# Spectral layer and two feed-forward layers on one core: the second mixing unit in three float32r passes, four weight conversions in the forward transform, odd groups reordered

## The chip, the cores and the metric

The kernel runs on one core of a Trainium2 chip. The metric is the device time of one execution in microseconds (us); a program that is run several times is told by the median.

## What is computed

```python
X = np.fft.rfft(x, axis=1)                       # x: (2, 3008, 256), float32
Yr = Xr @ w_r - Xi @ w_i + b_r
Yi = Xr @ w_i + Xi @ w_r + b_i
Yr, Yi = soft_threshold(Yr, 0.01), soft_threshold(Yi, 0.01)
y = np.fft.irfft(Yr + 1j * Yi, n=3008, axis=1)   # (2, 3008, 256) -> 6016 tokens
h = y @ w_in1;  y = (h * sigmoid(1.702 * h)) @ w_out1     # w_in 256x2048
h = y @ w_in2;  y = (h * sigmoid(h)) @ w_out2             # w_out 2048x256
```

The four feed-forward weights arrive as 64-bit floats; the kernel reads them as 64-bit integers and turns them into 32-bit floats itself.

## The kernel before, in words

Everything is 32-bit arithmetic. A matrix product on TensorE is made in one of two ways. *Full precision* multiplies float32 by float32 and appears as two records for one matmul. *Three passes* splits both operands into a rounded float32r part (hi) and the rest (lo) and adds hi·hi, hi·lo and lo·hi, one record each.

**Forward transform.** The input is folded by symmetry into sums and differences before it is multiplied with cosine and sine matrices. Sixteen *groups* (`groups`, numbers 0 to 15) stand for (parity of the input q, batch b, matrix t): 0 to 3 are even rows with t 0 and 1, 4 to 11 odd rows with t 0 to 3 for both batches, 12 to 15 even rows with t 2 and 3. A raw tile of the input (512 KB, `load_raw`, L300; nine in pool `raw`, three more in pieces) gives two *half sums* by a wide add of VectorE (`halves`, L313, 128x512; `keep` for even rows, `lv` for odd ones), and each of these two folded tiles (`fold`, L332, 128x256, narrow adds; some are combined once more at L346). `fwd_mm` (L394) or `fwd_pair` (L428) multiplies, `fwd_evac` moves the result from PSUM to the tiles xt: by ScalarE copies (L446), for groups 12 to 15 by a ScalarE copy eo (L450) and four VectorE adds (L461, L462). `fold` runs three groups ahead of the products.

**Mixing.** Twelve *units* (`mids`, 0 to 11) multiply xt by the weights w_r and w_i. Units below the table entry n32 (2 before) use full precision (L572); the others use three passes (L575), with the weights split into wh and wl (L556, L557, just behind the forward transform) and each unit's xt split into xh (a ScalarE cast, L507) and xl (a ScalarE product with -1, L503, to which a DMA of the GpSimd queue adds xt, L504), both made by `xsplit`. A bias row is added by one more matmul (L578). VectorE and ScalarE combine and threshold the result (L584 to L618).

**Inverse transform** (L394 as psi, `inv_post`), then two feed-forward layers in blocks of 1024 tokens, eight groups to a block: L876 multiplies with w_in, the activation runs on ScalarE (L879), L848 multiplies with w_out. At a change of block `xsums` and `xprep` make the seven operand combinations of the next block from yt; L796 is one of them, a VectorE subtraction that reads yt.

**Conversion of a weight.** A piece is loaded as raw 64-bit values (L162, L163; pool buffer `raw`, one), ScalarE takes the upper halves (cv_c, L180; one buffer), VectorE makes five bit operations (L185 to L189), a DMA of the GpSimd queue adds the low part (L190), and then the next raw load is issued. `window` puts ScalarE's step in the program, `pump` the rest. When a later window finds a converted piece, it *places* it: four small VectorE sums (L218 to L221) and hi/lo splits on ScalarE and by DMA (L105 to L107). Table entries say where windows stand: `tf` in the forward transform by group, `tm` in the mixing by unit, `ti` in the inverse transform by step; `pl` lists the steps of the inverse transform that place a held piece. Before, ten pieces are converted ahead of the feed-forward layers: three, six and one.

The order on every engine is that of the program text; a table `CFG` at the top sets who does what and when.

```python
        if g == 10:
            xsplit(N('n32'), 1)
        if g in N('tf'):
            tick(N('tf').count(g))
```

Of the kernel before, what the change touches and what calls it, by code (L numbers as in the profile page):

```python
# [9 lines left out]
F32 = mybir.dt.float32  # L10
CFG = {'lv0': 'V', 'lv': 'V', 'dd0': 'VPVVPPPPPVVP', 'dd': 'V', 'ths': 'VVVVPV', 'thf': 'V', 'ivf': 'V', 'cva': 'P', 'pol': 'PPPP', 'pil': 'P', 'mvl': 'PVVP', 'xl': 'V', 'xse': 'V', 'gl': 'VPPPPPPP', 'tf': [6, 10, 13], 'tm': [0, 2, 4, 6, 8, 10], 'ml': [], 'pk': 6, 'ti': [3], 'pi': 4, 'pl': [1, 4, 8, 10, 13], 'kb': [0, 1, 1, 1, 1, 1, 1, 0], 'kr': [0, 1, 0, 1, 0, 1, 1, 0], 'fa': 3, 'xp': [2, 4, 4, 5], 'xq': [1, 4, 1], 'xs': 4, 'xi': [7, 7, 9, 10, 10, 11, 8], 'xsi': 9, 'xo': (0, 1, 6, 2, 3, 4, 5), 'xd': (0, 1, 4, 6), 'ca': 4, 'tl': True, 'fwd': 'all', 'rest0': 'all', 'rest1': 'all', 'last1': 'all', 'inv': 'all', 'mid': 'all', 'last0': 'all', 'thm': 'A', 'gl0': 'PVPVVVPV', 'gl2': 'PPPPPPPP', 'gl3': 'PPPPPPPV', 'xl0': 'VVVVVPV', 'xl1': 'V', 'pre': 13, 'pre2': 0, 'yd': 6, 'lvb': 6, 'mlp': 'all', 'pr': 'V', 'pf': 'V', 'eo': '0111', 'n32': 2, 'li': [3, 5, 7], 'lii': [0], 'xa': 4, 'nhb': 6, 'ddb': 6, 'mlp1': 'all', 'mlp2': 'all'}
# [45 lines left out]
def spectral_mlp_kernel(ctx, tc, xin, mfwd, minv, wc, bias, w_in1, w_out1, w_in2, w_out2, outT):  # L57
# [60 lines left out]
    m_tiles = {}  # L118
    m_order = [("f", q, t) for q, t in ((0, 0), (0, 1), (1, 0), (1, 1), (1, 2), (1, 3), (0, 2), (0, 3))] + [("i", q, t) for q in range(2) for t in (0, 2)]

# [48 lines left out]
    def cv_bits(raw, n):  # L169
        w = raw.bitcast(U32).rearrange("p (n t) -> p n t", t=2)  # L170
        hf = raw.bitcast(F32).rearrange("p (n t) -> p n t", t=2)[:, :, 1]
        c = cv_p.tile([P, 2 * CU], F32, tag="c", name="cv_c", bufs=1)
        if n < 4:
            a = cv_p.tile([P, 2 * CU], F32, tag="a", name="cv_a", bufs=3)
        elif n == 4:
# [17 lines left out]
        return a, c  # L193
# [85 lines left out]
    m0_p = opened("m0", "left", 4)  # L279
    raw_p = opened("raw", "left", 3)  # L280
    lv_p = opened('lv', 'left', N('lvb'))
    xs_p = opened("xs", "left", 18)
    groups = [(0, b, cs) for b in range(B) for cs in range(2)]
    groups += [(1, b, t) for b in range(B) for t in range(4)]
    groups += [(0, b, 2 + cs) for b in range(B) for cs in range(2)]
# [16 lines left out]
    def halves(q, b, j, cs):  # L302
# [6 lines left out]
        else:  # L309
            lv = lv_p.tile([P, 2, D], F32, tag="lv", name="lv")  # L310
        lvs[q, b, cs, j] = lv
# [3 lines left out]
    def fold(g):  # L315
# [6 lines left out]
        for j in range(NJ):  # L322
            if t == 0:
                halves(q, b, j, 0)
            lv = lvs[q, b, cs, j]
# [23 lines left out]
    def fold_pair(g):  # L349
        q, b, _ = groups[g]  # L350
        for j in range(NJ):
# [15 lines left out]
    def prep_wc():  # L367
# [156 lines left out]
    for g, (q, b, t) in enumerate(groups):  # L524
# [244 lines left out]
    def xsums(l, i):  # L769
# [3 lines left out]
        E('xse', 1).tensor_sub(b12, b22, b12)  # L773

    def xprep(l, i, k, part=3):

# [7 lines left out]
        if part & 2:  # L784
# [79 lines left out]
    def group(l, i, p, hook):  # L864
# [116 lines left out]
    for at, (l, i, p) in enumerate(seq):  # L981
# [10 lines left out]
        def hook(h):  # L992
            if more:
                if h == 1:
                    xprep(*nxt, 0)
                if h == 3:
                    xprep(*nxt, 1)
                    xprep(*nxt, 2)
                    xprep(*nxt, 3, 1)
                if h == 4:  # L1000
                    xprep(*nxt, 3, 2)
            if p == 0 and (l, i) != (0, 0):
                for x in {1: (4,), 3: (6, 5)}.get(h, ()):
                    xprep(l, i, x)
# [169 lines left out]
```

## Time and profile before

| | |
|---|---|
| median of 3 runs | 1150.15 us (1149.65 to 1151.89) |
| profiled execution | 1149.84 us |
| its span, first to last instruction | 1148.0 us |
| TensorE busy (matmul) | 1138.8 us, 99% |
| ScalarE, VectorE, GpSimd busy | 774.1, 615.5, 475.9 us |
| forward transform until | about 59.6 us |
| mixing | about 59.6 to 130.6 us |
| inverse transform | about 130.6 to 172.8 us |
| feed-forward layers | the rest |

A row of the timeline gives start, duration, engine, line and operation; several instructions of one kind are merged with their count. In square brackets stands how long the engine was idle before and what ended that.

### The profile page before, as it was taken

Reading aid. Unit: us, or ns where it says so; the run is one execution under the profiler, and the core shown is the slowest. Engines: PE = TensorE matmul, PEld = TensorE weight load, DVE = VectorE, ACT = ScalarE, POOL = GpSimd, SP = SyncE. Lnnn points to the kernel's source line nnn. Section 1 sums busy time; section 2 is a strip of 40 time slices with the busy share of each in tenths; the row PEclk is TensorE's granted clock in tenths of the full one; section 3 lists DMA queues with packets and bytes.
Section 4 is the critical chain, followed back from the end, with each engine's and each line's share of the span. In section 5 each row is a group of like instructions: output and inputs, shape, how many; then the busy total and the mean of one; then the engine's idle time right before and its main releaser. Section 6 shows DMA issues by size and latency. Waiting matters only on the chain.

```text
span 1148.0 us, 14644 instructions
## 1 busy us (share of the span) xinstructions
PE 1138.8 (99%) x5094; PEld 946.3 (82%) x5094; DVE 615.5 (54%) x1015; ACT 774.1 (67%) x1445; POOL 475.9 (41%) x410
## 2 busy tenths in 40 slices
PE   8999999999999999999999999999999999999998
PEld 6768987878888888888889878888888888888897
DVE  8889997764565465564554633533523523523422
ACT  2587357877677676686677776765765866757655
POOL 0253164443444444444447646433334433344333
PEclk9999999999999999999999999999999999999999
DMA  8699494431121212112211000010000100100100
GB/s 306 176 185 238 114 161 86 105 72 37 49 62 37 74 37 59 52 38 74 52 41 37 28 28 19 1 38 1 20 18 1 37 1 1 38 1 1 37 1 33
DMA packets 39852, 68.69 MB, mean 60 GB/s; under 512 B 3681, under 2 KB 16225, under 8 KB 39778
## 3 DMA queue, kind: packets, MB, share of 16 engines
q1 hardware_dynamic: 26306, 45.51, 12.2%
q0 software_dynamic: 13472, 22.24, 11.4%
q8 instruction: 40, 0.66, 0.2%
q14 instruction: 34, 0.28, 0.1%
HBM read 35.15 MB, written 10.35 MB: 40 GB/s over the span
## 4 chain that ended last, share of the span: by engine, by line
PE 93%; DVE 2%; ACT 2%; issue 1%; DMA 1%; SPq 0%; POOL 0%; DVEq 0%; ACTq 0%; POOLq 0%
PE o L848 43%; PE x L876 37%; PE psm L575 5%; PE psi L394 4%; PE psf L394 3%; PE psm L572 1%; ACT yt L879 1%; DMA xr<-in_x 1%; ACT g L881 0%; DVE keep L313 0%; DVE tmp L796 0%; ACT yt L895 0%; ACT x L783 0%; DVE x L790 0%; SPq L485 0%
## 5 line engine op out<-in xcount | busy, mean ns | idle before, releaser
L886 POOL TENSOR_TENSOR g<-yt,g 128x512 fp32r<-128x512 f32 (+1 forms) x282 | 363.6, 1301 | 498.2 <-PE x L876 306.3
L848 PE MATMUL o<-g,wo 128*128 128x512 f32 (+1 forms) x2304 | 559.7, 385 | 0.0
L876 PE MATMUL x<-x,wi 128*128 128x512 f32 (+1 forms) x2016 | 498.9, 386 | 2.0 <-ACT yt L895 1.1
L848 PEld LDWEIGHTS o<-g,wo 128*128 128x128 f32 x2304 | 432.5, 188 | 80.6
L876 PEld LDWEIGHTS x<-x,wi 128*128 128x128 f32 x2016 | 377.5, 188 | 77.1 <-ACT yt L895 3.2
L879 ACT ACTIVATE yt<-yt 128x512 f32<-128x512 f32 (+1 forms) x288 | 179.1, 622 | 264.2 <-DVE yt L926 217.3
L881 ACT CAST g<-yt 128x512 fp32r<-128x512 f32 (+1 forms) x384 | 235.0, 612 | 12.2
L926 DVE TENSOR_TENSOR yt<-yt,x 128x512 f32<-128x512 f32 (+1 forms) x96 | 64.8, 675 | 217.7 <-PE x L876 217.3
L898 DVE TENSOR_TENSOR yt<-yt,x 128x512 f32<-128x512 f32 (+1 forms) x96 | 65.0, 677 | 175.0 <-ACT yt L895 173.1
L886 DVE TENSOR_TENSOR g<-yt,g 128x512 fp32r<-128x512 f32 (+1 forms) x102 | 70.0, 686 | 71.9 <-ACT g L881 71.9
L190 POOL DMA_DIRECT2D cv_a<-cv_c x32 | 28.1, 878 | 112.4 <-DVE cv_c L189 106.0
L930 DVE TENSOR_TENSOR yt<-yt,x 128x512 f32<-128x512 f32 (+1 forms) x96 | 64.9, 676 | 0.0
L790 DVE TENSOR_TENSOR x<-yt,x 128x512 fp32r<-128x512 f32 (+1 forms) x55 | 47.6, 866 | 31.5 <-ACT x L783 31.5
L895 ACT COPY yt<-x 128x512 f32<-128x512 f32 (+1 forms) x96 | 54.9, 572 | 1.7 <-DVE tmp L796 0.9
L879 ACT ACTIVATE yt<-x 128x512 f32<-128x512 f32 (+1 forms) x96 | 56.0, 584 | 0.0
L916 ACT COPY yt<-x 128x512 f32<-128x512 f32 (+1 forms) x96 | 55.9, 582 | 0.1
L914 ACT COPY yt<-x 128x512 f32<-128x512 f32 (+1 forms) x96 | 54.9, 572 | 1.4 <-PE x L876 1.4
L394 PE MATMUL psi<-m,f 128*128 128x188 f32 (+3 forms) x224 | 45.2, 357 | 0.0
L394 PEld LDWEIGHTS psi<-m,f 128*128 128x128 f32 x224 | 37.6, 190 | 5.5
L394 PE MATMUL psf<-m,xf 128*128 128x190 f32 (+2 forms) x176 | 36.2, 367 | 1.4 <-ACT xt L446 0.8
L394 PEld LDWEIGHTS psf<-m,xf 128*128 128x128 f32 x176 | 29.6, 190 | 8.3 <-ACT xt L446 1.3
L783 ACT CAST x<-yt 128x512 fp32r<-128x512 f32 (+1 forms) x59 | 36.4, 617 | 0.0
(120 smaller groups left out, 804.8 us busy)
## 6 DMA issues: line engine op xcount, KB each, us to landing
raw<-in_wi SPq DMA_DIRECT2D x32, 256.0 KB, 3.6
cv_a<-cv_c POOLq DMA_DIRECT2D x32, 256.0 KB, 5.0
raw<-in_wo SPq DMA_DIRECT2D x16, 512.0 KB, 3.9
xl<-xt POOLq DMA_DIRECT2D x20, 256.0 KB, 8.0
out_t<-yt SPq DMA_DIRECT2D x20, 256.0 KB, 2.0
raw<-in_x SPq DMA_DIRECT2D x9, 512.0 KB, 5.6
wi<-tmp POOLq DMA_DIRECT2D x8, 256.0 KB, 4.7
w_in<-cv_a SPq DMA_DIRECT2D x8, 256.0 KB, 2.0
```

The source lines that it names most:

```text
L394: nc.tensor.matmul(ps, hi[:, c : c + P], m[:, k, :w], start=i == 0, stop=i == last)
L575: nc.tensor.matmul(t, st, mv, start=n == 0 and k == 0, stop=n == 3 and grp == 1 and k == 2)
L848: nc.tensor.matmul(acc[h, mm], st, mv, start=first and k == 0, stop=last and k == 2)
L876: nc.tensor.matmul(ps, st, mv, start=first and m == 0, stop=m == 2, skip_group_check=True)
L879: nc.scalar.activation(g, g if src is None else src, func)
L881: nc.scalar.copy(gh, g)
L886: eng.tensor_sub(gl, g, r32(gh))
L895: nc.scalar.copy(y1, X)
L898: nc.vector.tensor_add(y1, y1, Y)
L916: nc.scalar.copy(y3, X)
L926: nc.vector.tensor_add(y2, y2, X)
L930: nc.vector.tensor_add(y3, y3, Z)
```

## The change

- `n32` goes from 2 to 1: unit 1 is made in three passes; its xl is made at group 10, and unit 2's xl and unit 1's xh behind wh and wl.
- `tf` goes from [6, 10, 13] to [6, 10, 12, 14], `ti` from [3] to []: four conversions in the forward transform, six in the mixing, none in the inverse transform. `pl` goes from [1, 4, 8, 10, 13] to [1, 4, 8, 9, 11, 13].
- Groups 4 to 11 run with t in the order 0, 2, 1, 3, and the matrices are loaded so. The half sums of t = 0 and t = 1 are made in the group that first uses them; the second is written over its raw tile. Pool `raw` has 5 buffers for 3, `lv` 3 for 6. Raw tiles are loaded ahead of the matrices, the ninth at group 4.
- The bias' lower part is written in place.
- At a change of block one subtraction (`xfifth`, before L796) moves ahead of the add that completes y3; the table of Silu is loaded by an instruction of its own.

```diff
-    m_order = [("f", q, t) for q, t in ((0, 0), (0, 1), (1, 0), (1, 1), (1, 2), (1, 3), (0, 2), (0, 3))] + ...
+    m_order = [("f", q, t) for q, t in ((0, 0), (0, 1), (1, 0), (1, 2), (1, 1), (1, 3), (0, 2), (0, 3))] + ...
...
-    raw_p = opened("raw", "left", 3)
-    lv_p = opened('lv', 'left', N('lvb'))
+    raw_p = opened("raw", "left", 5)
+    lv_p = opened('lv', 'left', 3)
...
-    groups += [(1, b, t) for b in range(B) for t in range(4)]
+    groups += [(1, b, t) for b in range(B) for t in (0, 2, 1, 3)]
...
-            lv = lv_p.tile([P, 2, D], F32, tag="lv", name="lv")
+            lv = raws[q, b, j][1] if cs else lv_p.tile([P, 2, D], F32, tag="lv", name="lv")
...
-            if t == 0:
-                halves(q, b, j, 0)
+            if q == 1 and t < 2:
+                halves(q, b, j, t)
...
-            if t == 0:
-                halves(q, b, j, 1)
-                del raws[q, b, j]
-                if (q, b) == (0, 0):
-                    load_raw()
...
-    load_raw(3)
+    load_raw(6)
+    load_m()
+    load_m()
+    load_raw(2)
     fold_pair(0)
-    load_m()
     fold_pair(2)
-    load_m()
...
-    load_raw(3)
...
+        if g == 4:
+            load_raw()
...
-            xsplit(N('n32'), 1)
+            xsplit(1, 1)
...
     nc.vector.tensor_sub(wl, wc_s, r32(wh))
+
+    xsplit(2, 1)
+    xsplit(1, 0)
...
-    hold.insert(2, hold.pop())
+    hold[2:] = hold[4:] + hold[2:4]
...
+    def xfifth(l, i, src=None):
+        (b11, _), (b21, _) = xhalves(i)
+        nc.vector.tensor_sub(xtmp[0], b21, b11 if src is None else src)
...
-            if k == 3:
-                nc.vector.tensor_sub(xtmp[0], b21, src)
+            if k == 3 and not begun:
+                xfifth(l, i, src)
...
         nc.vector.tensor_add(y2, y2, X)
+        hook(7)
         g22 = gate(1, 1, y2)
...
+                if h == 7:
+                    xfifth(*nxt)
...
+            if (l, i, p, h) == (1, 0, 0, 1):
+                nc.scalar.preload_act_table(AF.Silu)
```

How the order moves, at three places. First ScalarE at the end of the forward transform. Of the kernel before, from the third conversion's first step (`cv_c<-raw_548`) to the fourth's (`cv_c<-raw_630`):

```order
L180 ACTIVATE cv_c<-raw_548 128x512
L105 ACTIVATE wi_609<-cv_a 128x384
L107 CAST wi_609<-cv_a 128x384
L105 ACTIVATE wi_609<-tmp 128x512
L107 CAST wi_609<-tmp 128x512
L450 COPY eo<-psf 128x2x188 x3
L556 CAST wh<-wc_s 128x1536
L503 ACTIVATE xl<-xt_303 128x512
L503 ACTIVATE xl<-xt_304 128x512
L507 CAST xh<-xt_97 128x512
L507 CAST xh<-xt_98 128x512
L180 ACTIVATE cv_c<-raw_630 128x512
```

Of the change, from the evacuation of groups 12 and 13 on (line numbers are those of the changed file; `cv_c<-raw_607` is the fourth conversion, xt_97 and xt_98 belong to unit 2, xt_95 and xt_96 to unit 1):

```order
L443 COPY eo<-psf 128x2x188 x2
L180 ACTIVATE cv_c<-raw_607 128x512
L105 ACTIVATE wi_642<-cv_a 128x384
L107 CAST wi_642<-cv_a 128x384
L105 ACTIVATE wi_642<-tmp 128x512
L107 CAST wi_642<-tmp 128x512
L443 COPY eo<-psf 128x2x188 x2
L550 CAST wh<-wc_s 128x1536
L496 ACTIVATE xl<-xt_97 128x512
L496 ACTIVATE xl<-xt_98 128x512
L500 CAST xh<-xt_95 128x512
L500 CAST xh<-xt_96 128x512
```

The fourth conversion's first step stood behind wh, xl and xh; now it stands ahead of them and of the last two eo copies.

Second, VectorE at the same place. Of the kernel before, the evacuation of group 15, wl, and then the fourth conversion:

```order
L461 TENSOR_TENSOR xt_310<-psf,eo 128x256
L462 TENSOR_TENSOR xt_314<-psf,eo 128x2x60
L436 TENSOR_TENSOR xt_312<-eo,psf 128x256
L436 TENSOR_TENSOR xt_314<-eo,psf 128x2x60
L557 TENSOR_TENSOR wl<-wc_s,wh 128x1536
L218 TENSOR_TENSOR tmp<-cv_a 128x128
L219 TENSOR_TENSOR tmp<-cv_a 128x128
L220 TENSOR_TENSOR tmp<-tmp,cv_a 128x128
L221 TENSOR_TENSOR tmp<-cv_a,tmp 128x128
L185 TENSOR_SCALAR cv_c<-cv_c 128x512
L186 TENSOR_SCALAR cv_c<-cv_c 128x512
L187 SCALAR_TENSOR_TENSOR cv_a<-raw_630,cv_c 128x512
```

Of the change, the end of the fourth conversion, groups 14 and 15, and wl:

```order
L187 SCALAR_TENSOR_TENSOR cv_a<-raw_607,cv_c 128x512
L188 TENSOR_SCALAR cv_c<-cv_a 128x512
L189 SCALAR_TENSOR_TENSOR cv_c<-raw_607,cv_c 128x512
L454 TENSOR_TENSOR xt_303<-psf,eo 128x256
L455 TENSOR_TENSOR xt_307<-psf,eo 128x2x60
L429 TENSOR_TENSOR xt_305<-psf,eo 128x256
L429 TENSOR_TENSOR xt_307<-psf,eo 128x2x60
L454 TENSOR_TENSOR xt_304<-psf,eo 128x256
L455 TENSOR_TENSOR xt_308<-psf,eo 128x2x60
L429 TENSOR_TENSOR xt_306<-eo,psf 128x256
L429 TENSOR_TENSOR xt_308<-eo,psf 128x2x60
L551 TENSOR_TENSOR wl<-wc_s,wh 128x1536
```

wl stood ahead of the fourth conversion; now it stands behind it and behind the two evacuations.

Third, VectorE at the first change of block (the two adds into yt complete y2 and y3 of the last group of a block). Of the kernel before:

```order
L926 TENSOR_TENSOR yt<-yt,x 128x512
L930 TENSOR_TENSOR yt<-yt,x 128x512
L886 TENSOR_TENSOR g<-yt,g 128x512
L790 TENSOR_TENSOR x<-yt,x 128x512
L796 TENSOR_TENSOR tmp<-yt 128x512
L898 TENSOR_TENSOR yt<-yt,x 128x512
```

Of the change:

```order
L927 TENSOR_TENSOR yt<-yt,x 128x512
L774 TENSOR_TENSOR tmp<-yt 128x512
L932 TENSOR_TENSOR yt<-yt,x 128x512
L887 TENSOR_TENSOR g<-yt,g 128x512
L791 TENSOR_TENSOR x<-yt,x 128x512
L899 TENSOR_TENSOR yt<-yt,x 128x512
```

The subtraction into tmp (L796, now L774) goes ahead of y3's add and the two instructions behind that.

## Rows read from the trace of the kernel before

**Rows 1.** The page's head: TensorE's busy time; granted clock of forty slices, in tenths.

```profile
PE 1138.8 (99%) x5094; PEld 946.3 (82%) x5094; DVE 615.5 (54%) x1015; ACT 774.1 (67%) x1445; POOL 475.9 (41%) x410
...
PEclk9999999999999999999999999999999999999999
```

**Rows 2.** TensorE's waits over the span: us in total, times, longest us.

```profile
PE x L876 <- ACT yt L895: 1.1, 3, 0.7
PE warm L472 <- DVE neglam L474: 1.1, 1, 1.1
```

**Rows 3.** The chain that ended last, in the mixing: start us, us, what.

```profile
59.59 3.43 PE psm L572 x8
63.25 6.87 PE psm L572 x16
...
73.79 2.77 PE psm L575 x12
76.79 5.45 PE psm L575 x24
```

**Rows 4.** Timeline of ScalarE, 55 to 68 us.

```profile
55.00 0.68 ACT L180 ACTIVATE cv_c<-raw 128x512 f32<-128x512 f32 x1 [2.54 <-DMA raw<-in_wi]
...
57.44 0.83 ACT L450 COPY eo<-psf 128x376 f32<-128x376 f32 x2
...
60.04 1.48 ACT L556 CAST wh<-wc_s 128x1536 fp32r<-128x1536 f32 x1
...
62.47 1.12 ACT L507 CAST xh<-xt 128x512 fp32r<-128x512 f32 x2
64.64 0.68 ACT L180 ACTIVATE cv_c<-raw 128x512 f32<-128x512 f32 x1 [1.05 <-DMA raw<-in_wi]
...
67.08 0.58 ACT L584 COPY us<-psm 128x512 f32<-128x512 f32 x1
```

**Rows 5.** Timeline of VectorE, third conversion to wl.

```profile
55.71 0.43 DVE L185 TENSOR_SCALAR cv_c<-cv_c 128x512 f32<-128x512 f32 x1
...
58.43 0.42 DVE L461 TENSOR_TENSOR xt<-psf,eo 128x256 f32<-128x256 f32 x1
...
59.47 0.42 DVE L461 TENSOR_TENSOR xt<-psf,eo 128x256 f32<-128x256 f32 x1
...
61.55 1.76 DVE L557 TENSOR_TENSOR wl<-wc_s,wh 128x1536 fp32r<-128x1536 f32 x1
```

**Rows 6.** Timeline of VectorE, folds of group 4 to conversion 2.

```profile
18.78 0.69 DVE L313 TENSOR_TENSOR lv<-raw 128x512 f32<-128x512 f32 x1
...
35.86 0.42 DVE L185 TENSOR_SCALAR cv_c<-cv_c 128x512 f32<-128x512 f32 x1
...
41.19 2.08 DVE L332 TENSOR_TENSOR xf<-keep 128x256 f32<-128x256 f32 x6
44.92 0.29 DVE L218 TENSOR_TENSOR tmp<-cv_a 128x128 f32<-128x128 f32 x1 [1.65 <-DMA cv_a<-cv_c]
...
45.86 0.42 DVE L185 TENSOR_SCALAR cv_c<-cv_c 128x512 f32<-128x512 f32 x1
```

**Rows 7.** Landing times: the page's DMA issues; the tile xl, 30 to 140 us.

```profile
raw<-in_x SPq DMA_DIRECT2D x9, 512.0 KB, 5.6
...
DMA to landing us min/median/max: 3.4/8.0/10.6
```

**Rows 8.** Timelines of TensorE, VectorE and ScalarE at two changes of block.

```profile
255.05 1.79 DVE L796 TENSOR_TENSOR tmp<-yt 128x512 f32<-128x512 f32 x1
...
256.93 0.59 ACT L895 COPY yt<-x 128x512 f32<-128x512 f32 x1 [0.85 <-PE x L876]
...
257.57 0.96 PE L876 MATMUL x<-x,wi 128*128 128x512 f32 x3 [0.69 <-ACT yt L895]
...
658.95 0.96 PE L876 MATMUL x<-x,wi 128*128 128x512 f32 x3 [0.26 <-ACT yt L895]
...
663.04 1.97 PE L876 MATMUL x<-x,wi 128*128 128x512 f32 x6 [0.70 <-ACT yt L916]
```

More of the change, by code (lines that the diff above doesn't have):

```diff
@@ L10 @@
 F32 = mybir.dt.float32
-CFG = {'lv0': 'V', 'lv': 'V', 'dd0': 'VPVVPPPPPVVP', 'dd': 'V', 'ths': 'VVVVPV', 'thf': 'V', 'ivf': 'V', 'cva': 'P', 'pol': 'PPPP', 'pil': 'P', 'mvl': 'PVVP', 'xl': 'V', 'xse': 'V', 'gl': 'VPPPPPPP', 'tf': [6, 10, 13], 'tm': [0, 2, 4, 6, 8, 10], 'ml': [], 'pk': 6, 'ti': [3], 'pi': 4, 'pl': [1, 4, 8, 10, 13], 'kb': [0, 1, 1, 1, 1, 1, 1, 0], 'kr': [0, 1, 0, 1, 0, 1, 1, 0], 'fa': 3, 'xp': [2, 4, 4, 5], 'xq': [1, 4, 1], 'xs': 4, 'xi': [7, 7, 9, 10, 10, 11, 8], 'xsi': 9, 'xo': (0, 1, 6, 2, 3, 4, 5), 'xd': (0, 1, 4, 6), 'ca': 4, 'tl': True, 'fwd': 'all', 'rest0': 'all', 'rest1': 'all', 'last1': 'all', 'inv': 'all', 'mid': 'all', 'last0': 'all', 'thm': 'A', 'gl0': 'PVPVVVPV', 'gl2': 'PPPPPPPP', 'gl3': 'PPPPPPPV', 'xl0': 'VVVVVPV', 'xl1': 'V', 'pre': 13, 'pre2': 0, 'yd': 6, 'lvb': 6, 'mlp': 'all', 'pr': 'V', 'pf': 'V', 'eo': '0111', 'n32': 2, 'li': [3, 5, 7], 'lii': [0], 'xa': 4, 'nhb': 6, 'ddb': 6, 'mlp1': 'all', 'mlp2': 'all'}
+CFG = {'lv0': 'V', 'lv': 'V', 'dd0': 'VPVVPPPPPVVP', 'dd': 'V', 'ths': 'VVVVPV', 'thf': 'V', 'ivf': 'V', 'cva': 'P', 'pol': 'PPPP', 'pil': 'P', 'mvl': 'PVVP', 'xl': 'V', 'xse': 'V', 'gl': 'VPPPPPPP', 'tf': [6, 10, 12, 14], 'tm': [0, 2, 4, 6, 8, 10], 'ml': [], 'pk': 6, 'ti': [], 'pi': 4, 'pl': [1, 4, 8, 9, 11, 13], 'kb': [0, 1, 1, 1, 1, 1, 1, 0], 'kr': [0, 1, 0, 1, 0, 1, 1, 0], 'fa': 3, 'xp': [2, 4, 4, 5], 'xq': [1, 4, 1], 'xs': 4, 'xi': [7, 7, 9, 10, 10, 11, 8], 'xsi': 9, 'xo': (0, 1, 6, 2, 3, 4, 5), 'xd': (0, 1, 4, 6), 'ca': 4, 'tl': True, 'fwd': 'all', 'rest0': 'all', 'rest1': 'all', 'last1': 'all', 'inv': 'all', 'mid': 'all', 'last0': 'all', 'thm': 'A', 'gl0': 'PVPVVVPV', 'gl2': 'PPPPPPPP', 'gl3': 'PPPPPPPV', 'xl0': 'VVVVVPV', 'xl1': 'V', 'pre': 13, 'pre2': 0, 'yd': 6, 'lvb': 6, 'mlp': 'all', 'pr': 'V', 'pf': 'V', 'eo': '0111', 'n32': 1, 'li': [3, 5, 7], 'lii': [0], 'xa': 4, 'nhb': 6, 'ddb': 6, 'mlp1': 'all', 'mlp2': 'all'}
 NUM = dict(li=[5, 6, 7, 8], n32=2, pk=4, ydp=2, lii=[1, 3], xd=(), ml=[], pl=[], xo=range(7), pi=6, nhb=6, tf=[5, 9, 13], tm=[1, 3, 5, 7, 9, 11], ti=[0, 2, 4, 6, 8, 10, 12, 14, 14, 15, 15], kb=[2] * 8, kr=1, fa=3, fe=2, pm=0, nf=4, lvb=6, ddb=8, ivb=1, eob=1, fsb=6, f1=3, f2=0, fm=[7, 8, 9], fi=[1, 1, 2, 2], pre=13, pre2=1, yd=3, psh=0, ie=[12], xp=[1, 3, 4, 5], xq=[1, 2, 2], xs=5, nw=4, xi=[14, 14, 15, 15], xsi=13, rw=2, ca=4, cc=2, tb=1, tmn=1)
@@ L118, in spectral_mlp_kernel @@
     m_tiles = {}
-    m_order = [("f", q, t) for q, t in ((0, 0), (0, 1), (1, 0), (1, 1), (1, 2), (1, 3), (0, 2), (0, 3))] + [("i", q, t) for q in range(2) for t in (0, 2)]
+    m_order = [("f", q, t) for q, t in ((0, 0), (0, 1), (1, 0), (1, 2), (1, 1), (1, 3), (0, 2), (0, 3))] + [("i", q, t) for q in range(2) for t in (0, 2)]
     def load_m():
@@ L172, in cv_bits @@
         c = cv_p.tile([P, 2 * CU], F32, tag="c", name="cv_c", bufs=1)
-        if n < 4:
+        if n < 3:
             a = cv_p.tile([P, 2 * CU], F32, tag="a", name="cv_a", bufs=3)
-        elif n == 4:
+        elif n == 3:
             a = cv_p.tile([P, 2 * CU], F32, tag="ld", name="cv_a", bufs=1)
@@ L358, in fold_pair @@
             del raws[q, b, j]
-            if b == 0:
-                load_raw()
     def load_wc():
@@ L372, in prep_wc @@
         nc.scalar.copy(bias_hl, bias_f)
-        nc.vector.tensor_sub(bias_lo, bias_f[0:1], r32(bias_hl[0:1]))
-        nc.gpsimd.dma_start(out=bias_hl[1:2], in_=bias_lo)
+        nc.vector.tensor_sub(bias_f[0:1].bitcast(F32R), bias_f[0:1], r32(bias_hl[0:1]))
+        nc.gpsimd.dma_start(out=bias_hl[1:2], in_=bias_f[0:1].bitcast(F32R))
     xt = {}
@@ L476, in spectral_mlp_kernel @@
     bias_hl = wc_p.tile([P, 2 * D], F32R, name="bias_hl")
-    bias_lo = wc_p.tile([1, 2 * D], F32R, name="bias_lo")
     bias_f = wc_p.tile([P, 2 * D], F32, name="bias_f")
```

## Prediction, made before the changed kernel ran

> **What bounds the kernel now.** I read the page's head first. TensorE is busy for 1138.8 of 1148.0 us, and its granted clock is at the top in all forty slices, so at the upper of its two levels, 2.4 GHz [rows 1]. Its own waits come next: they add up to a few us, and the longest are 1.1 us at the start and 0.7 at a change of block [rows 2]. So the time falls only where TensorE gets fewer passes or loses one of these waits, and it rises by whatever makes TensorE wait. The other engines matter through their order: ScalarE and VectorE take their work as it is queued, and the idle times in brackets show each of them standing still when its next instruction is not ready [rows 4, 6]. The profiled execution took 1149.84 us, 0.31 below the median of the runs (1150.15). I make the sum against the former and add the 0.31 at the end. A difference of 0.2% (2.3 us) is about what a measurement of this kernel can tell from no change.
>
> **Unit 1 in three passes.** In the mixing, half of a full-precision unit (8 records, four matmuls) takes 3.43 us, so a unit 6.86; 24 float32r passes take 5.45 [rows 3]. Unit 1 gets shorter by 6.86 - 5.45 = 1.41 us. Unit 0 started at 59.59, its second half at 63.25, and it ended at 63.25 + 3.43 = 66.68. There unit 1 now needs the weights' halves wh and wl and its own xh and xl. Before, the first unit in passes began at 73.79 [rows 3], and wl was complete at 61.55 + 1.76 = 63.31 [rows 5]. If all else stayed, there would be 3.4 us to spare. It doesn't stay.
>
> **The fourth conversion stands in front of wh and wl.** A conversion is a ring: ScalarE's first step (cv_c), five VectorE steps, an accumulating DMA and meanwhile the load of the next raw weights. There is one buffer for raw and one for cv_c, so the next first step waits for both transfers. The ring sets its own pace: VectorE's part began at 35.86 and 45.86 [rows 6] and 55.71 [rows 5], steps of 10.0 and 9.85 us. The fourth first step ran at 64.64, 9.64 after the third, when ScalarE had stood idle 1.05 us for the raw load [rows 4]. Before, the evacuations of groups 14 and 15, wh and wl had been issued ahead of that wait. Now that step comes first, in the order shown above, and they are behind it.
>
> When does it run now? Let T be its start.
> - Conversion 1 on VectorE comes after the folds of groups 4 to 9. These began at 18.78, and conversion 1 followed at 35.86. Three of their wide adds (0.69 us) and two narrow ones (0.35: 2.08 for six) move behind it [rows 6]: 35.86 - 2.07 - 0.70 = 33.1. But group 8 now needs the ninth raw tile, which has no free buffer until group 7's first fold, six wide and fourteen narrow adds after 18.78, at 27.8. Such loads take 5.6 us to land [rows 7], so it is there at 33.4, and VectorE wants it eight wide and twenty narrow adds after 18.78, at 31.3. The start lies between 33.1 (no late tile) and 35.2 (2.1 late); I take 34.5, for fewer transfers run beside this load than beside most.
> - The same three wide and two narrow adds (2.8 us) now stand between conversions 1 and 2, where VectorE was idle for 1.65 us [rows 6]. The step of 10.0 grows by 1.1: conversion 2 at 45.6, against 45.86. What was won is given back.
> - From there the ring is as it was. So I take T = 64.64 as before; the bounds are 63.0 (from 33.1) and 65.1 (from 35.2).
>
> Behind T, on VectorE: 0.71 us until it begins (55.00 on ScalarE [rows 4] to 55.71), the conversion's five steps 2.72 (55.71 to 58.43), two evacuations 2.08 (59.47 to 61.55), wl 1.76 [rows 5]: T + 7.27 = 71.91. On ScalarE: first step and four splits 2.44 (64.64 to 67.08), two eo 0.83, wh and xl 2.43 (60.04 to 62.47), xh 1.12 [rows 4]: T + 6.82 = 71.46. So TensorE, done with unit 0 at 66.7, starts unit 1 at about 71.5 and its second pass, which reads wl, at 71.9: **a wait of about 5 us where there was none.** Unit 2 starts at 71.91 + 5.45 = 77.36, where it started at 73.79 [rows 3]: **+3.6 us** with the 1.41 already in it (bounds +1.9 and +4.0).
>
> **What sits behind it.** Unit 2's xl is now made after wh: ScalarE has written its first half at about T + 5.2, and such a transfer lands 3.4 to 10.6, in the middle 8.0 us later [rows 7], at about 77.9; unit 2's third pass wants it at 77.36 + 0.46 = 77.8. The second half comes some 0.9 us later and is wanted 1.4 later. So from 0 to 2.5 us; I take **+0.4**, since the middle landing just meets it. Later units have the same few us less to spare, and a first wait repairs it for the rest, so I add nothing for them. The PSUM banks don't bind: a unit's two banks come back four units later, three units of 5.45 us after it ends.
>
> **The forward transform.** Group 4's inputs come sooner by two wide adds, about 1.3 us, and all groups behind it can move ahead as much. This is worth nothing: unit 1 waits for T, which doesn't move. The earlier raw loads, the swapped matrices and the bias written in place cost nothing for the same reason; were the wait gone, the 1.3 us would count. Unit 0 needs group 12's banks, free when its evacuation has followed conversion 3: 58.43 + 1.04 = 59.5, beside a start of 59.59 before. No cost.
>
> **Inverse transform.** One conversion less, one weight placed more. TensorE has no wait there now [rows 2], so nothing is to be won.
>
> **The changes of block.** At 257.57, 658.95 and 663.04 TensorE waited 0.69, 0.26 and 0.70 us for ScalarE's copies. The copy of 256.93 could start only when VectorE's L796 had read the same part of yt, at 255.05 + 1.79 = 256.84 [rows 8]. The change puts this subtraction three places earlier on VectorE. The copy then starts when ScalarE comes to it, about 0.9 us sooner (its idle time there is 0.85), which takes away 0.69 and 0.26 and, through the same chain on ScalarE, most of 0.70. The table load goes one place ahead, where ScalarE is busy either way: nothing. I take **-1.5**; bounds 0 and -1.65.
>
> **Sum:** +3.6 + 0.4 - 1.5 = +2.5 us on 1149.84, and 0.31 to the median: **1152.6 us**. The bounds together give 1150.4 and 1156.7.
>
> **Rivals.**
> 1. *The clock falls in the wait* (0.20). No row has a wait of 5 us ahead of matmuls, only 1.1 at most, and the clock stayed up; so the rows speak neither way for a longer one. If TensorE comes back at 1.2 GHz, passes take twice as long: from 0 to 5.45 us, all of unit 1; half of it gives +2.7, so 1155.3. The Trainium skill ("TensorE: Matmul & The Clock Gate", section "HAM oscillation — how this bites in real kernels") says that a long gap between groups of matmuls drops the engine to its lower clock and that the next group then starts slow. By that rule this rival would be the forecast; no row here has such a gap. I leave it below the likeliest.
> 2. *The wait never comes* (0.08), the case on the other side. It decides at T = 66.9 - 7.3 = 59.6: were the fourth first step able to run by then, wl would be ready for unit 1, and the 1.41 us and the 1.5 of the block changes would be kept: 1149.84 - 2.9 + 0.31 = 1147.2, and with the 1.3 of the forward transform 1145.9. For it: transfers that land nearly 2 us sooner in each of three turns, because the raw loads of the input are out of the way earlier. Against: the three turns in the rows agree to 0.4 us.
> 3. *The ring is quicker by part* (0.17): with T between 62 and 63 the wait costs 1 to 2 us net, and the block changes pay for it: about 1150, no change.
>
> **How the numbers follow.** The forecast has 0.55; its own range is 1151.0 to 1155.0, and about two thirds of it lie over 1152.45. Slower by over 0.2%: 0.36 of that and all of rival 1, 0.56. Within 0.2%: the other 0.19 and rival 3, 0.36. Faster: rival 2, 0.08. The range for 8 in 10 leaves out rival 2 and the upper end of rival 1: 1149.6 to 1156.2.
>
> **What would show it.** Right: TensorE idle for about 5 us from 67 to 72, released by ScalarE's xh or VectorE's wl; ScalarE idle just before the fourth cv_c at about 64.6, with eo and wh behind it; unit 2's first pass near 77.4; no waits at those block changes. Wrong: wl complete before 67, which would be rival 2; a granted clock below the top behind 67, which would be rival 1. If the mixing ends later by much more than unit 2 starts later, the xl transfers were late again and again, and my 0.4 was the wrong term.

## The result, and the profile after

The changed kernel took 1157.33 us in the median of four runs (1156.56 to 1157.91); the kernel before, run beside it, 1150.14. The ratio is 1.0061, with a 95% interval from 1.0048 to 1.0074: slower by 7.2 us, beyond the 0.2% that can be told from no change, and 1.1 us above the upper end of the forecast range. The side was right and the size was not. The profiled execution took 1157.91 us, its span 1156.1.

The head of the page, after (TensorE's busy time; granted clock of forty slices):

```profile
PE 1140.2 (99%) x5102; PEld 948.3 (82%) x5102; DVE 608.8 (53%) x1015; ACT 777.4 (67%) x1449; POOL 472.1 (41%) x412
...
PEclk9989999999999999999999999999999999999999
```

Against [rows 1], the third slice now has an 8 in its clock. TensorE's waits, after (us in total, times, longest us):

```profile
PE psm L572 <- ACT xh L500: 5.5, 1, 5.5
...
PE psi L387 <- PE psi L387: 0.6, 1, 0.6
PE psi L387 <- DVE rt L720: 0.6, 1, 0.6
...
PE x L877 <- ACT yt L896: 0.3, 2, 0.2
PE x L877 <- ACT yt L917: 0.3, 1, 0.3
```

One wait of 5.5 us has come up in the mixing. Two of 0.6 are new in the inverse transform. At the changes of block, the 1.1 of [rows 2] has shrunk to 0.3, and the 0.70 behind the other copy [rows 8] to 0.3. VectorE's last sum of the mixing, that of unit 11 (first line before, second line after):

```profile
130.74 0.69 DVE L586 TENSOR_TENSOR sd<-us,psm 128x512 f32<-128x512 f32 x1 [0.96 <-PE psm L575]
...
140.37 0.69 DVE L583 TENSOR_TENSOR sd<-us,psm 128x512 f32<-128x512 f32 x1
```

The inverse transform starts at 130.47 and 137.45. So this sum came 0.27 us behind its start before, when VectorE had waited for TensorE, and comes 2.92 us behind it now, when VectorE waited for nothing. TensorE's timeline around unit 1, after:

```profile
59.91 3.70 PE L569 MATMUL psm<-wc_s,xt 128*128 128x512 f32 x8 [0.93 <-ACT eo L443]
...
63.69 3.60 PE L569 MATMUL psm<-wc_s,xt 128*128 128x512 f32 x8
72.81 0.80 PE L572 MATMUL psm<-wh,xh 128*128 128x512 f32 x1 [5.53 <-ACT xh L500]
73.88 0.80 PE L572 MATMUL psm<-wl,xh 128*128 128x512 f32 x1 [0.27 <-DVE wl L551]
...
75.75 0.63 PE L572 MATMUL psm<-wh,xl 128*128 128x512 f32 x1
76.18 0.53 PE L572 MATMUL psm<-wh,xh 128*128 128x512 f32 x1
76.55 0.39 PE L572 MATMUL psm<-wl,xh 128*128 128x512 f32 x1
```

From 74.47 to 76.18 unit 1's passes begin 0.43 us apart and take up to 0.63; from 76.55 on they begin 0.23 apart and take 0.39. The windows of the same execution say why (us, TensorE busy, granted clock, DMA share, GB/s):

```profile
66.00:68.00 2.00, 1.28 (x3) 1.00 0.01 5
68.00:70.00 2.00, 0.00 (x0) 0.91 0.36 59
70.00:72.00 2.00, 0.00 (x0) 0.50 1.03 141
72.00:74.00 2.00, 0.92 (x2) 0.50 1.05 236
74.00:76.00 2.00, 2.00 (x5) 0.50 1.09 241
76.00:78.00 2.00, 2.00 (x9) 0.89 1.16 210
```

The clock fell to its lower level, 1.2 GHz, inside the wait, at about 69.6, and stayed there until about 76.4, for the first 3.6 us of passes (estimates from the 0.91 and the 0.89 of the windows that hold the two ends). ScalarE's timeline holds what unit 1 waited for; [rows 4] show the same stretch before:

```profile
66.56 0.68 ACT L180 ACTIVATE cv_c<-raw 128x512 f32<-128x512 f32 x1 [6.32 <-DVE tmp L218]
...
68.99 0.84 ACT L443 COPY eo<-psf 128x376 f32<-128x376 f32 x2
69.72 1.48 ACT L550 CAST wh<-wc_s 128x1536 fp32r<-128x1536 f32 x1
...
72.15 1.13 ACT L500 CAST xh<-xt 128x512 fp32r<-128x512 f32 x2
```

ScalarE stands idle for 6.3 us with eo, wh and xh queued behind the fourth cv_c. It starts at T = 66.56, not at 64.64. VectorE shows where the ring lost this, to be laid beside [rows 5, 6]:

```profile
33.32 0.69 DVE L313 TENSOR_TENSOR lv<-raw 128x512 f32<-128x512 f32 x1 [0.88 <-DMA raw<-in_x]
...
35.46 0.42 DVE L185 TENSOR_SCALAR cv_c<-cv_c 128x512 f32<-128x512 f32 x1
...
46.84 0.42 DVE L185 TENSOR_SCALAR cv_c<-cv_c 128x512 f32<-128x512 f32 x1
...
56.63 0.29 DVE L218 TENSOR_TENSOR tmp<-cv_a 128x128 f32<-128x128 f32 x1 [4.90 <-DMA cv_a<-cv_c]
...
57.67 0.43 DVE L185 TENSOR_SCALAR cv_c<-cv_c 128x512 f32<-128x512 f32 x1
```

The ninth raw tile came late as feared (0.88), and conversions 1, 2 and 3 began on VectorE at 35.46, 46.84 and 57.67 where 34.5, 45.6 and, as before, 55.7 were forecast.

The span splits into four stretches that add up (from the starts of unit 0, of the inverse transform, of the first x, which is the first product of the feed-forward layers, and of the last matmul, each on TensorE):

| stretch | before | after | difference |
|---|---|---|---|
| up to unit 0 | 59.43 | 59.91 | +0.48 |
| unit 0 to the inverse transform | 71.04 | 77.54 | +6.50 |
| inverse transform to the first x | 41.92 | 44.41 | +2.49 |
| first x to the last matmul | 970.97 | 969.45 | -1.52 |
| behind it | 4.64 | 4.79 | +0.15 |

The sum is +8.1, as the spans (1148.0 and 1156.1); the medians differ by 7.2, since the profiled execution of the change was the longest of its four. The first stretch isn't evidence: in these runs unit 0 started between 58.4 and 61.3 us, even in kernels with one and the same forward transform (59.81 and 61.29). In the later of these two, TensorE had two stops of 1.1 and 0.6 us between 22 and 24.2 us, and the clock stood at 0.50 from 26 to 28; in the other it had stops of 0.8 and 0.6, and the clock stayed at 1.00. So executions are compared below from unit 0 on.

### The profile page after: what moved, and what is told of

Same layout as the page of the kernel before. It is cut to its first block, busy times and chain, and to the rows that moved or that the text cites. A ratio compares the mean times of both kernels' runs of the same rounds, so it can differ in the third digit from the quotient of the medians.

```text
span 1156.1 us, 14679 instructions
## 1 busy us (share of the span) xinstructions
PE 1140.2 (99%) x5102; PEld 948.3 (82%) x5102; DVE 608.8 (53%) x1015; ACT 777.4 (67%) x1449; POOL 472.1 (41%) x412
## 4 chain that ended last, share of the span: by engine, by line
PE 86%; DVE 2%; issue 2%; ACT 2%; DMA 1%; POOL 0%; DVEq 0%; POOLq 0%; ACTq 0%
PE o L849 43%; PE x L877 38%; PE psm L572 5%; ACT yt L880 1%; DMA yt<-ac 0%; DMA cv_a<-cv_c 0%; DVE ac L719 0%; PE psi L387 0%; DVE x L791 0%; DVE rt L720 0%; ACT g L882 0%; ACT yt L896 0%; ACT x L784 0%; PE psm L575 0%; ACT yt L752 0%
## 5 line engine op out<-in xcount | busy, mean ns | idle before, releaser
L887 POOL TENSOR_TENSOR g<-yt,g 128x512 fp32r<-128x512 f32 (+1 forms) x282 | 358.2, 1285 | 503.4 <-PE x L877 307.4
L791 DVE TENSOR_TENSOR x<-yt,x 128x512 fp32r<-128x512 f32 (+1 forms) x55 | 43.1, 783 | 36.1 <-ACT x L784 36.1
L880 ACT ACTIVATE yt<-x 128x512 f32<-128x512 f32 (+1 forms) x96 | 56.1, 584 | 0.0
L572 PE MATMUL psm<-wh,xh 128*128 128x512 f32 x88 | 35.0, 398 | 5.5 <-ACT xh L500 5.5
L180 ACT ACTIVATE cv_c<-raw 128x512 f32<-128x512 f32 x32 | 21.7, 677 | 25.9 <-DVE tmp L218 13.2
```

Source lines behind the costliest of these rows:

```text
L572: nc.tensor.matmul(t, st, mv, start=n == 0 and k == 0, stop=n == 3 and grp == 1 and k == 2)
L880: nc.scalar.activation(g, g if src is None else src, func)
L887: eng.tensor_sub(gl, g, r32(gh))
```

## The experiments

Each ratio is to the kernel before, run on the same chip in the same job. The table has the profiled execution of each kernel. VectorE's last sd is its sum for unit 11; "mixing" runs from unit 0's start to the inverse transform's.

| kernel | mixing, us | last sd behind the transform's start | transform to first x | first x behind last sd | ratio, interval |
|---|---|---|---|---|---|
| before | 71.04 | 0.27 | 41.92 | 41.65 | 1 |
| the change | 77.54 | 2.92 | 44.41 | 41.49 | 1.0061 [1.0048, 1.0074] |
| three conversions forward | 69.62 | 3.08 | 44.52 | 41.44 | 0.9984 [0.9975, 0.9993] |
| fourth conversion behind the splits | 77.98 | 5.2 | 46.67 | 41.4 | 1.0061 [1.0047, 1.0075] |
| filler of six (profile of a second run) | 77.23 | 5.0 | 46.42 | 41.4 | 1.0079 [1.0066, 1.0092], first run |
| filler of eleven | 79.18 | 3.60 | 46.25 | 42.65 | 1.0084 [1.0069, 1.0100] |
| changes of block only | 71.04 | 0.70 | 42.15 | 41.45 | 0.9983 [0.9974, 0.9992] |
| unit 1 and changes of block | 69.62 | 3.63 | 45.09 | 41.46 | 0.9987 [0.9978, 0.9996] |
| last conversion in the inverse transform | 78.52 | 0.27 | 41.92 | 41.65 | 1.0042 [1.0030, 1.0055] |
| the change, folds on GpSimd | 78.63 | 1.37 | 42.28 | 40.91 | 1.0033 [1.0021, 1.0046] |
| unit 1, blocks, folds on GpSimd | 69.62 | 0.33 | 41.92 | 41.59 | 0.9974 [0.9966, 0.9983] |
| three forward, folds on GpSimd | 69.61 | 2.52 | 43.49 | 40.97 | 0.9974 [0.9963, 0.9985] |
| three forward, five in the mixing | 69.79 | 1.62 | 44.27 | 42.65 | 0.9974 [0.9962, 0.9987] |

**Three conversions in the forward transform.** The change, without its fourth conversion ahead of unit 1:

```diff
-... 'tf': [6, 10, 12, 14], ... 'ti': [], ... 'pl': [1, 4, 8, 9, 11, 13], ...
+... 'tf': [6, 10, 13], ... 'ti': [3], ... 'pl': [1, 4, 8, 10, 13], ...
```

The buffers of cv_a and the order of `hold` go back with it.

> The change, but with three conversions in the forward transform (after groups 6, 10, 13), six in the mixing and one in the inverse transform, as before. Theory A (the fourth conversion's place made the loss: ScalarE and VectorE had it in front of wh, wl, xh): TensorE's wait of 5.5 us ahead of unit 1 is gone, the clock stays up, the inverse transform has no waits; unit 2 starts near 72.4 instead of 80.65; 1146 to 1148 us. Rival B (unit 1 in three passes is late by its own operands, wherever the fourth conversion stands): a wait of some us ahead of unit 1 or 2 stays, 1150 us or more.

Measured: 1149.42 us. Unit 1 follows unit 0 with no wait, at a granted clock of 1.00, and the mixing is 1.42 us shorter than before. So the wait is the fourth conversion's, as the forecast had it, and the three passes save what was forecast (1.41). But the time fell by only 0.0016 of 1150, about 1.8 us, less than expected, and this the changes of block alone can pay for. What the mixing won is lost in the inverse transform. TensorE's waits there, in this kernel (none in [rows 2]):

```profile
PE psi L387 <- DVE rt L429: 0.7, 1, 0.7
...
PE psi L387 <- DVE rt L720: 0.6, 1, 0.6
```

**The fourth conversion behind the splits.** The change, with that conversion issued after unit 1's operands:

```diff
-... 'tf': [6, 10, 12, 14], ...
+... 'tf': [6, 10, 12], ...
...
     xsplit(2, 1)
     xsplit(1, 0)
+    tick(1)
```

> The change with four conversions ahead of unit 0's thresholds as it has them, but the fourth one issued behind wh, wl, xl of unit 2 and xh of unit 1 instead of ahead of the evacuation of groups 14 and 15. Theory A (order alone): like three conversions in the forward transform, 1146 to 1148 us; VectorE not late at the end of the mixing, no waits in the inverse transform. Rival C (the ring of ten conversions ahead of the inverse transform is itself too much for VectorE): the wait ahead of unit 1 is gone, but waits of 1 to 3 us stay in the inverse transform, 1149 to 1151 us.

Measured: 1157.92 us, as slow as the change, and both theories missed. Unit 1 ran without a wait. The wait moved one conversion on, as ScalarE's timeline shows:

```profile
77.73 0.66 ACT L180 ACTIVATE cv_c<-raw 128x512 f32<-128x512 f32 x1 [6.60 <-DMA raw<-in_wi]
...
81.68 1.12 ACT L500 CAST xh<-xt 128x512 fp32r<-128x512 f32 x2
```

and TensorE's behind it:

```profile
82.33 0.50 PE L573 MATMUL psm<-wh,xh 128*128 128x512 f32 x1 [3.77 <-ACT xh L500]
```

Here too the clock fell behind the stop: it was 0.81 from 82 to 84 us, 0.50 to 86 and 0.84 to 88. The ring turns in about 11 us (66.51 to 77.73 here). Wherever a cv_c is issued before its turn is up, whatever is queued behind it on ScalarE waits.

**A filler in the wait.** The change, with dummy matmuls ahead of unit 1, six in the first kernel and eleven in the other:

```diff
             n = 0
+            if (i, grp) == (1, 0):
+                for _ in range(6):
+                    nc.tensor.matmul(t, ones_f, wc_s[:, 0, : 2 * D], start=True, stop=True)
```

> The change with six full-precision matmuls of ones and wc_s issued ahead of unit 1's first pass, into the bank that unit 1 then overwrites; they fill some 5.1 of the 5.9 us. Nothing that the output needs is changed. Theory D (the lower clock cost what the passes of unit 1 lost, 1.3 us, on the path): granted clock 1.00 throughout, unit 2 starts at about 79.3 instead of 80.65, time 1.3 us below the change, 1156.0. Rival E (VectorE's lateness sets the end, so the clock costs nothing): unit 2 earlier by 1.3, but the waits in the inverse transform longer by as much, 1157.3 as the change.

Measured: 1159.7 us. The profile read here is of one more run of the same kernel, which took 1158.9 us:

> The change plus six fp32 matmuls (2.6 us of TensorE at the 0.43 us that one takes in unit 0) on the bank of unit 1's first half ahead of its first pass; their result is overwritten by the pass that starts the sum, so nothing of the output changes. It was 2.4 us slower than the change, where 0 or -1.3 was expected. Theory A (the six wait for something on their own, a bank or their weights, and hold unit 1 back): unit 1's first pass starts later than 72.81, by 1 to 3 us, and the profile names what the first of the six waits for. Theory B (nothing is held back, the loss lies later): unit 1 starts at 72.8 and unit 2 at 79.3 to 80.7, and the 2.4 us appear in the inverse transform or behind it.

This second expectation has a slip: such a matmul is two instructions of 0.43 us, so six take 5.15 us, as the first one has it, and not 2.6. Unit 1's first pass came 12.86 us behind unit 0's start, against 12.90 in the change: nothing held it back, and theory B stands. The clock stayed at 1.00. Of what that gave, only 0.3 us was left in the mixing, because the faster passes met operands that weren't ready (0.9 for wl, 0.5 for xh and xl), and VectorE was 5.0 us late at the inverse transform. There, a stop of 1.5 us without a releaser in the profile came on top, as in the kernel with the fourth conversion behind the splits; what it is stays open.

> The same with eleven fp32 matmuls, 4.7 us, nearly the whole wait of 5.5 us. Theory A (the clock falls because TensorE stands idle): granted clock 1.00 from 66 to 80 us, unit 1's passes 0.23 us apart from the first, unit 2 starts 1.3 us earlier than the change's 80.65; the time is that of the change less 1.3 (1156.0) if the inverse transform gives nothing back. Theory B (the drop has another cause, such as the ramp of traffic at 70 us): 0.50 again from 70 to 76 us and 1157.3 or more.

Measured: 1160.41 us. The eleven took 9.6 us, more than the wait, and pushed unit 1 back by 3.3 us (its first pass 16.24 behind unit 0's start). The clock, in this kernel's windows (columns as above):

```profile
70.00:72.00 2.00, 2.00 (x6) 1.00 1.04 139
72.00:74.00 2.00, 2.00 (x6) 1.00 1.06 249
74.00:76.00 2.00, 2.00 (x7) 1.00 1.11 248
76.00:78.00 2.00, 2.00 (x10) 1.00 1.13 204
```

The same traffic as in the change and no fall of the clock: it was TensorE standing idle. From unit 1's first pass to the inverse transform it took 62.94 us, like 62.92 with three conversions forward; the change took 64.64. So the low clock, with the 0.27 us for wl, costs the change 1.7 us. The clock is as theory A has it, and the time isn't: the filler was too long, and in the inverse transform a stop of 2.4 us without a releaser came on top, behind which the clock did fall (0.74 from 166 to 168 us, 0.50 to 170).

**The changes of block alone.** The kernel before with `xfifth`, its hook and the earlier load of the Silu table, and nothing else:

```diff
+        hook(7)
         g22 = gate(1, 1, y2)
...
+                if h == 7:
+                    xfifth(*nxt)
...
+            if (l, i, p, h) == (1, 0, 0, 1):
+                nc.scalar.preload_act_table(AF.Silu)
```

> The kernel before with the change at the block borders alone: the subtraction ahead of y3's add, and the Silu table loaded by its own instruction. Forecast of my sum: 1.5 us below before, 1148.6, waits of 0.69, 0.26 and 0.70 us at 257.6, 659.0 and 663.0 gone or below 0.3. Rival: the waits move to the next instruction, 1150.1.

Measured: 1148.29 us, 1.9 below before. The waits at those places are gone but for 0.3 us.

**Unit 1 in three passes, with the changes of block.** On the kernel before; conversions, loads and groups stay:

```diff
-            xsplit(N('n32'), 1)
+            xsplit(1, 1)
...
     nc.vector.tensor_sub(wl, wc_s, r32(wh))
+    xsplit(2, 1)
+    xsplit(1, 0)
```

with `'n32': 1` and the edit above.

> The kernel before with two of the change's parts: unit 1 in three passes with the x splits moved behind wl, and the fifth sum and the Silu table moved to the end of the block before; conversions, loads and the order of the groups stay. Theory A (TensorE's 1.4 us saved in unit 1 last to the end): start of the inverse transform 129.1 rather than 130.47, 1150.15 - 1.4 - 1.86 = 1146.9. Theory B (what the mixing gains is given back in the inverse transform, where VectorE ends no earlier): start of the inverse transform 129.1 or earlier, waits of psi on rt and sd of 1 us and more, full group of x at 175 as before; 1148.3, that of the kernel with the block change alone.

Measured: 1149.26 us, ratio 0.9987, no better than the changes of block alone (0.9983). The mixing is shorter by exactly 1.42 us and the inverse transform longer by 3.2. Theory B. VectorE's last sd came 73.25 us behind unit 0's start, where it came 71.31 before; it stood idle 2.1 and 1.05 us for conversions whose turns took 11.3 to 12.2 us. The ring turned no slower than before: from its fourth cv_c to its ninth it took 56.2 us, and 56.1 before. But its fourth cv_c stood 8.0 us behind unit 0's start, and 5.2 before; in the kernel with the changes of block alone, whose forward transform is that of before, it stood at 8.0 too. So, measured against before, VectorE's lateness was in the ring when unit 0 began, and the profile of before is a favourable one. Against the changes of block alone the last sd is 1.5 us later (71.74 there), 0.9 of it in the ring's turns; why those were slower isn't settled.

**The last conversion back in the inverse transform.** The change, with four conversions forward but five in the mixing:

```diff
-... 'tm': [0, 2, 4, 6, 8, 10], ... 'ti': [], ...
+... 'tm': [0, 2, 4, 6, 8], ... 'ti': [3], ...
```

> The change with five conversions in the mixing and the last in the inverse transform (four in the forward transform stay). Theory A (the 2.3 us that the inverse transform lost are VectorE's, which left the mixing 2.7 us later behind TensorE than before because of the sixth conversion): wait of 5.5 us and clock of 0.50 ahead of unit 1 as in the change, unit 2 at 80.6, start of the inverse transform 137.4; sd of the last unit 2 us earlier than 140.37, first rt 7 us behind the transform's start rather than 9.4, and the full group of x at 182.0 rather than 184.27; 1155.0. Theory B (the lateness is not the sixth conversion's): 184.3 and 1157.3 as in the change; the conversion in the inverse transform then adds its own 1 to 2 us of VectorE and PE waits there: 1158 to 1159.

Measured: 1155.43 us. The wait and the low clock ahead of unit 1 are as in the change (the mixing is 1.0 us longer than there, for more of unit 1's passes ran under the lower clock). VectorE, at the end of the mixing:

```profile
137.62 0.69 DVE L583 TENSOR_TENSOR sd<-us,psm 128x512 f32<-128x512 f32 x1 [1.24 <-PE psm L572]
```

It now waits for TensorE, as before the change, and the inverse transform is back at 41.92 us to the hundredth. Theory A.

**Folds on GpSimd.** If VectorE's lateness is the cause, taking any work off VectorE must help. The subtraction that makes f for units 6 to 10 goes to GpSimd, in three kernels:

```diff
-'thf': 'V'
+'thf': 'VVVVVVVVVVVVVPVPVPVPVPVV'
```

First the change with this edit alone:

> The change with one kind of VectorE work given to GpSimd: the subtraction that folds th into f for units 6 to 10 (five instructions of 0.60 us each). TensorE's work and the wait ahead of unit 1 stay. Theory A (the first x group starts 41.4 to 41.7 us behind VectorE's last unit sum sd, because VectorE, 2.7 us late at the end of the mixing, sets the pace of the inverse transform): last sd up to 3.0 us earlier than 140.4, at 137.6; inverse transform 42.0 us long instead of 44.4; first x at 179.4 instead of 181.86; 1155.0. Theory B (the lateness comes from the chain of conversions, whose pace a lighter VectorE does not change, or GpSimd's folds delay the transfers that GpSimd issues): last sd at 140, first x at 181.9 or later, 1157.3 or more.

Measured: 1153.62 us, 0.0028 of the time (3.2 us) less than the change; the profiled execution was the longest of its five, 1155.91. The last sd came 1.55 us less late and not 2.8. Of this, 1.1 us are TensorE's, whose mixing was longer by as much; behind unit 0's start the sd came only 0.45 us earlier, 80.00 for 80.45, since VectorE still waited for conversions. The inverse transform took 42.28 us. Next, the kernel with unit 1 in three passes and the changes of block:

> The kernel before with unit 1 in three passes and the two edits at the changes of block, and the same five folds on GpSimd. Theory A: last sd 2.5 us earlier than 133.1, inverse transform 42.1 us instead of 45.1, first x at 171.6 instead of 174.5, 0.9987 of before less 2.5 us: 1146.2 of 1150.15. Theory B: last sd at 133, first x 174.5, 1148.6.

Measured: 1147.56 us, ratio 0.9974. The folds on GpSimd, from the groups of instructions between 100 and 140 us (count, busy us and mean ns, idle time before):

```profile
L614 POOL TENSOR_TENSOR f<-th 128x512 f32<-128x512 f32 x5 | 7.1, 1425 | 3.9 <-DVE th L602 3.7
```

They cost GpSimd 1.43 us each, in place of 0.60 on VectorE, in time that GpSimd had. VectorE's own folds that ran beside them took 2.18 us once and 0.72 to 0.76 four times, where 0.68 is usual. The last sd stood 0.33 us behind the transform's start and not 3.63, and the transform took 41.92 us. Theory A, and in this profile the whole 1.42 is kept. Not all of that is owed to the folds. Behind the ninth cv_c the last sd came 7.9 us instead of 9.0, so they saved 1.1 us. The other 2.2 are the ring's, whose ninth cv_c stood 62.0 us behind unit 0's start instead of 64.2: unit 0 started 1.5 us later in this execution (61.29), and the ring stood 0.7 earlier. Last, the kernel with three conversions forward:

> The change with three conversions in the forward transform, six in the mixing and one in the inverse transform, and the same five folds on GpSimd. Theory A: last sd at 128.9 instead of 131.6, inverse transform 42.1 us instead of 44.5, first x at 170.5 instead of 172.99, 1147.0 of 1150.15. Theory B: last sd 131.6, first x 173, 1149.4.

Measured: 1147.29 us, ratio 0.9974. Its last sd is less late by 0.56 us only, and the transform shorter by 1.0: theory A by half. Here too the last sd came 7.9 us behind the ninth cv_c instead of 9.0, but the ring stood 0.5 us later behind unit 0's start.

**Five conversions in the mixing, two in the inverse transform.** On the kernel with three conversions forward:

```diff
-... 'tm': [0, 2, 4, 6, 8, 10], ... 'ti': [3], ...
+... 'tm': [0, 2, 4, 6, 8], ... 'ti': [3, 7], ...
...
-    hold.insert(2, hold.pop())
```

> The change with three conversions in the forward transform, five in the mixing and two in the inverse transform. Theory A (what counts is VectorE's load up to the last sd): last sd 2.5 us earlier than 131.6, inverse transform 42 us plus what the second conversion costs there, which is 0 to 2.7 us of VectorE: first x at 170.4 to 173.1, 1146.9 to 1149.5. Theory B (the inverse transform is TensorE's own 42 us and something else delayed it): 1149.4 with waits of 1 to 3 us on the transform's rows, first x at 173 or later.

Measured: 1148.22 us, ratio 0.9974. The last sd is 1.5 us less late, but the first x follows it 42.65 us later, not 41.4: the second conversion costs 1.2 us there. This lies within theory A's span and says less than the folds do.

## Why the prediction was wrong, point by point

The wait, the three passes and the changes of block came as forecast in kind. The sum failed mainly in two terms that it put at nothing, the inverse transform (2.5 us) and the clock (1.7 us), and in the wait, which was 1.2 us too short.

- **The wait ahead of unit 1: right in place, short in size.** TensorE stood idle from 67.3 to 72.8 behind wh and xh, which stood behind the fourth cv_c. What failed is the step "From there the ring is as it was. So I take T = 64.64". T was 66.56, outside the bounds of 63.0 to 65.1. Behind T the working held: wl was complete at 72.07 + 1.76 = 73.83, 7.27 us after T, as forecast. Ahead of T, the late raw tile and the folds behind it took 1.0 us more than forecast, the step from conversion 1 to 2 another 0.3, and the step from 2 to 3 another 1.0, because the accumulating transfer kept VectorE waiting for 4.90 us. (Counted on from its own 45.6, the ring would have given 45.6 + 9.85 + 8.93 = 64.4, not 64.64.) The steps of 10.0 and 9.85 us were also those of one execution. In the kernel with the changes of block alone, whose forward transform is that of before, they were 11.0 and 11.7, and the fourth cv_c started at 67.87. With four conversions ahead of unit 1 it started at 65.3 to 66.6 in five profiles, above the bounds in each; how much of that is the change's stays open. Unit 0 was 0.5 late as well: it waited 0.93 us for eo, where "No cost" had been forecast. Unit 1's first pass came 12.90 us behind unit 0's start, against 6.70 without the fourth conversion: 6.2 us in place of about 5.0.
- **Three passes: right.** 1.41 forecast, 71.04 - 69.62 = 1.42 measured in two kernels.
- **The clock: rival 1 came true,** beside the wait and not instead of it. It cost 1.7 us in the change and 2.9 in the two other kernels with this wait (65.8 us from unit 1's first pass to the inverse transform, against 62.9). The rival's price, "half of it gives +2.7", was near. Its chance of 0.20 was too low, for the clock fell in all three kernels with this wait. The Trainium skill ("TensorE: Matmul & The Clock Gate", section "HAM oscillation — how this bites in real kernels") says that a long wait between groups of matmuls throttles the engine and that the next group starts slow. The trace agrees, with 0.50 from 70 to 76 us.
- **xl late: nothing.** 0.4 was taken (0 to 2.5); the profile of the change has no wait for xl. At the low clock the passes came to it later; with the filler of six, at 1.00, the wait for xl was 0.2.
- **The inverse transform: the step that failed outright.** "TensorE has no wait there now, so nothing is to be won" asked only what could be won. It lost 2.49 us: three stops, 1.4 us together in the rows, which cost more than they show, since passes that follow one another without a stop overlap there. The transform takes TensorE 41.92 us on its own, provided that VectorE's last sd is no more than some 0.3 us behind its start; otherwise the first x follows 41.4 to 41.7 us behind that last sd (40.9 to 41.6 with the folds moved; 42.65 in the two kernels with a second conversion or an unexplained stop of 2.4 us in the transform). In the kernel before, these two limits lie within some 0.2 us of each other. Both kernels issue six conversions in the mixing, but the sixth was the ninth of all before (cv_c at 120.7) and is the tenth now (130.7), a turn of the ring later; it put VectorE past the limit, as the run with the last conversion put back shows.
- **The changes of block: right.** -1.5 forecast; -1.9 in the runs with this part alone, a little beyond the bound of -1.65, and -1.52 in the table's fourth stretch.
- **The forward transform:** worth nothing here, as forecast, since unit 1 waited for T.

From unit 0 on, the parts close: +6.2 (wait) - 1.42 (passes) + 1.72 (clock) = +6.50 in the mixing, +2.49 in the inverse transform, -1.52 at the changes of block. Forecast were +3.6 with the passes in it, +0.4, 0 and -1.5.

Three versions beat both kernels, each with a ratio of 0.9974: unit 1 in three passes with the changes of block and five folds on GpSimd, and the change with three conversions forward, either with the same folds or with two conversions in the inverse transform. What all three leave out is the fourth conversion ahead of unit 1. Their intervals still overlap with that of the changes of block alone (0.9983).

## What to carry to other kernels

TensorE at 99% doesn't mean that it alone sets the pace: before a saving on the busiest engine is counted, look how long the next engine waits for it at the stage's end. Here VectorE waited 0.96 us ahead of its last sum in the one profile that was read, and not at all in the kernel with the changes of block alone, so a saving of 1.42 us had little to pass through. A start time that a ring of transfers sets is worth reading from more than one execution: the ring's fourth first step stood 5.2 us behind unit 0's start in one and 8.0 in another, with the same forward transform. An instruction with a long wait ahead of it costs the queue behind it: in an engine that takes its work in order, place it where its operand is due, and price every later turn of its ring as well. Where a change opens a stop of several us ahead of matmuls, price the fall of the clock as part of the forecast, not as a rival.

## What the hardware showed that was not expected

The same stop cost differently each time. In the change TensorE was idle for 5.53 us and the clock was back at about 76.4; with the last conversion in the inverse transform it was idle for 5.47, and the passes from 71.57 on ran under a clock that was still low at 76 to 78:

```profile
70.00:72.00 2.00, 0.43 (x1) 0.70 1.03 196
...
74.00:76.00 2.00, 2.00 (x6) 0.50 1.16 230
76.00:78.00 2.00, 2.00 (x6) 0.59 1.12 203
78.00:80.00 2.00, 2.00 (x10) 1.00 1.12 190
```

By an estimate from the windows that hold its ends, the lower clock lasted equally long in both, from 69.6 to 76.4 and from 70.8 to 77.6. What differed is when in the stop it began: 2.4 us after TensorE had gone idle in the change, 4.7 us in the other kernel. So 3.6 us of passes ran under it in the one and 6.1 in the other. A price of 1.7 or 2.9 us hangs on one and the same stop, and the runs don't tell what sets the moment of the fall.
